# Sliding-window attention and a feed-forward layer on one core: V loads behind the x transposes, q and k transposes before late x, first k loaded by ScalarE

## The chip, the core and the metric

The kernel runs on one core of a Trainium2 chip. Five engines each follow a list of instructions of their own and meet at semaphores: TensorE (PE: matrix products and transposes), ScalarE (ACT: activation functions, copies, casts), VectorE (DVE: element-wise work), GpSimd (POOL) and SyncE (SP). GpSimd, SyncE and ScalarE can also issue DMA transfers. The metric is device time in microseconds for one execution; the time before is 313.18 us, the median of three runs (313.08 to 313.22).

## What is computed

Attention over 8 batches of 8 heads with 576 tokens and 64 values per head, causal with a window of 128 and a bias that falls linearly with distance; its result is rearranged to 4608 tokens of 512 values and goes through two matrix products with g = h cos(h) between them.

```python
scores = scale * q @ k.T                       # per batch and head
bias = slopes * -abs(rel); mask = (rel >= 0) & (rel < 128)
attn = softmax(where(mask, scores + bias, -1e9))
x = (attn @ v).transpose(0, 2, 1, 3).reshape(4608, 512)
h = x @ w_in                                   # 512 -> 2048
out = (h * cos(h)) @ w_out                     # 2048 -> 512
```

## The kernel before

**Tiling and stages.** The 4608 tokens are cut into 9 chunks of 512 for the feed-forward layer. Attention is cut into units: eight for each batch, each a block of queries against itself and the block before it. Seven units of batch 0 run first. Then comes, for each chunk c, the first product (`moe1`, line 748; for chunk 0 `moe1_block`, line 773), 8 or 9 further units of attention (`attention`), and the second product (`moe2`, line 801). In the text, phase c is what is issued between chunk c's first product and its second. The units of phase c are the last one of batch c and the first seven of batch c+1. A unit's scores (line 557) go through an exponential (line 584) and a mask (603) to the product with V (lines 619 to 633), are normalised (656 to 670) into `xnat`, or into `xfirst` for a batch's first block and `xtail` for its last, and must then be transposed into `xT`, the operand of `moe1`.

**The x transposes.** A unit whose tokens are in the first four of a phase (the first two in phase 0) has its x transposed by a DMA on SyncE's queue (`x_dma`, lines 732 and 735); these are collected in the list `begin`. Of the rest, units whose tokens are needed only in the chunk after next ("late x") go through SyncE too; the others are transposed on TensorE (`x_pe`).

**Loads.** Batches 0 and 1 get q and k in pieces (`load_qk`, lines 366 and 377) that TensorE transposes (lines 493 and 498). From batch 2 on, q and k are loaded whole by GpSimd (`load_nat`, line 395, five transfers each for q and k) and transposed by two DMAs each on SyncE's queue (`dma_transposes`, lines 404 and 407; line 404 takes four blocks, line 407 the last half block). In phase c these transposes are for batch c+2, and come after the `begin` transposes; the loads of q and k for batch c+3 wait for them, since they use the same buffer. V of batch c+2 is loaded by GpSimd in five transfers (`load_v`, line 385) into one of two buffers. GpSimd's loads convert float32 to bfloat16 on the way; SyncE's and ScalarE's don't. The first piece of q is loaded as float32 by SyncE and cast by ScalarE or VectorE (line 372).

**What sets the order.** A planner (`Plan.schedule`) simulates the engines with the durations written at each operation (`occ`: the engine is held; `lat`: until the result is there) and at each step starts, for each engine, the ready operation with the smallest priority number, then the earliest in the program. Default priority is 5. The resulting order is fixed at build time for each engine; GpSimd's operations keep the order of the program. At run time each engine follows its list and waits on semaphores for what its next operation reads or overwrites. A planner's duration that is wrong thus changes orders, and not what is waited for. In `op`, a key in `r` makes the operation wait for the writer of that key.

The lines that make the order of V, and of the transposes, in a phase are these:

```python
begin = attention(every[done:done + n], c)
done += n
while next_v < B and done >= 8 * (next_v - 1):
    load_v(next_v)
    next_v += 1
...
    dma_transposes(next_t, begin)
```

Of the kernel before, what the change touches and what calls it, by code (L numbers as in the profile page):

```python
# [8 lines left out]
F32 = mybir.dt.float32  # L9
# [4 lines left out]
NBLK = 5  # L14
# [270 lines left out]
def bass_alibi_sliding__then__act_gcu_kernel(  # L285
# [8 lines left out]
    with ExitStack() as ctx:  # L294
# [4 lines left out]
        op = R.op  # L299
# [2 lines left out]
        w_out = sb("w_outb", [128, NFC, DMODEL])  # L302
        xT = sb("xT", [128, NPAIR, NTOK])
        gT = [sb(f"gT{i}", [128, NFC, CH]) for i in range(2)]
        qF = sb("qfirst", [128, 2, 256], F32)
        qC = sb("qcast", [128, 4, 2, 64])
        qB = {"q": sb("qrows", [128, 2, 1152]), "k": sb("krows", [128, 2, 1152])}
        qE = {"q": sb("qend", [128, 2, 128]), "k": sb("kend", [128, 2, 128])}
        nat = {"q": sb("qnat", [128, NBLK, H, D]), "k": sb("knat", [128, NBLK, H, D])}
# [50 lines left out]
        def load_qk(which, src, b, n=0):  # L360
            t0, rr, _ = PIECES[b][n]
            c0 = 64 * (t0 // 32)
            rows = bass.AP(src.tensor, src[b].offset + 64 * t0,
                           [[64 * rr, 32], [64 * S, H], [1, 64 * rr]])
            if b == 0 and n == 0 and which == "q":
                op("sp", [lambda e: e.dma_start(qF[:, :, :], rows)],
                   w=["qF"], dma="ldqf", occ=400, lat=750)
                i = qF[:, :, :].rearrange("p y (j d) -> p y j d", j=4)
                o = qC[:, :, :, :].rearrange("p j y d -> p y j d")
                op(("act", "dve"),  # L370
                   {"act": lambda e: e.activation(o, i, ACTF.Copy),
                    "dve": lambda e: e.tensor_copy(o, i)},
                   r=["qF"], w=piece_keys(which, b, n), occ={"act": 460, "dve": 330},
                   lat={"act": 560, "dve": 410}, pri=2)
                return
            o = qE[which][:, :, :] if t0 == 512 else qB[which][:, :, c0:c0 + 64 * rr]
            op("pool", [lambda e: e.dma_start(o, rows)],  # L377
               w=piece_keys(which, b, n), dma=f"ld{which}{n}", occ=750,
               lat={2: 600, 4: 1000 if n == 0 else 1050 if which == 'q' else 750,
                    8: 1800 if which == 'q' else 1300, 18: 2850}[rr])  # L380

        def load_v(b, order=range(NBLK)):
            for t in order:
                rows = 128 if t < 4 else 64
                op("pool", [lambda e, t=t, rows=rows: e.dma_start(  # L385
                    vp[b % 2][0:rows, t, :, 0:64],
                    v[b, :, 128 * t:128 * t + rows, :].rearrange("h p d -> p h d"))],
                   r=[("vinit", b % 2)], w=[("v", b % 2, t)], dma=f"ldv{b % 2}{t}",
                   occ=900, lat=7 * rows + (500 if b == 0 and t == 0 else 0))

        def load_nat(which, src, b):
            fns = []
# [7 lines left out]
        def dma_transposes(b, after):  # L400
            for which in ("q", "k"):
                t = tr[which][b % 2][:, :].rearrange("p (c k t) -> p c k t", c=NBLK, k=NPAIR)
                fns = [
                    lambda e, t=t, which=which: e.dma_start_transpose(  # L404
                        t[:, 0:4, :, :].rearrange("p c k t -> p (c k) t"),
                        nat[which][:, 0:4, :, :].rearrange("p c h d -> p (c h d)")),
                    lambda e, t=t, which=which: e.dma_start_transpose(
                        t[:, 4, :, 0:64],
                        nat[which][0:64, 4, :, :].rearrange("p h d -> p (h d)")),
                ]  # L410
                op("sp", fns, r=[("nat", which)] + ([("ktail", b % 2)] if which == "k" else []),
                   w=[("tr", which, b % 2)], dma=f"tr{which}{b % 2}", occ=4500, lat=6500,
                   after=after)

        def load_w_in(f0, f1):
            op("pool", [lambda e: e.dma_start(
# [11 lines left out]
        def constants():  # L428
            op("dve", lambda e: e.memset(zeros[:, :], 0.0), w=["zeros"], occ=60, pri=0)
            op("pool", lambda e: e.iota(dif[:, :, :], pattern=[[128, 2], [-1, 128]], base=-128,  # L430
                                        channel_multiplier=1,
                                        allow_small_or_imprecise_dtypes=True),
               w=["dif"], occ=360)

            op("dve", lambda e: e.tensor_scalar(ident[:, :], dif[:, 1, :], 0.0, None,
                                                ALU.is_equal), r=["dif"], w=["ident"],
               occ=170, lat=250, pri=0)
            for i, (edge, test) in enumerate([(-127.0, ALU.is_lt), (0.0, ALU.is_gt)]):
                op("dve", lambda e, i=i, edge=edge, test=test: e.tensor_scalar(
                    off[:, i, :], dif[:, i, :], edge, -1.0e6, test, ALU.mult),  # L440
                   r=["dif"], w=[("off", i)], occ=170, lat=250, pri=0)
            op("dve", lambda e: e.tensor_tensor(dif[:, :, :], dif[:, :, :], off[:, :, :], ALU.add),
               r=[("off", 0), ("off", 1)], w=["dif"], occ=350, lat=430, pri=0)
            for i in range(2):
                op("dve", lambda e, i=i: e.memset(vp[i][:, :, :, 64:65], 1.0), w=[("vinit", i)],
                   pri=1)
                op("dve", lambda e, i=i: e.memset(vp[i][64:128, 4, :, 0:64], 0.0),
                   w=[("vinit", i)], occ=270, pri=1)
            for i in range(NP):
                op("dve", lambda e, i=i: e.memset(P[i][:, 1024:1088], 0.0), w=[("P", i)], occ=90)  # L450
            op("dve", lambda e: e.memset(halfpi[:, :], math.pi / 2.0), w=["halfpi"], occ=60)
            for i in range(2):
                op("dve", lambda e, i=i: e.memset(
                    tr["k"][i][:, :].rearrange("p (k t) -> p k t", k=NPAIR)[:, :, 576:640], 0.0),
                   w=[("ktail", i)], occ=170)
# [23 lines left out]
        def qk_transposes(b, which, n, part, banks):  # L479
            t0, rr, groups = PIECES[b][n]  # L480
            jj = groups[2 * part:2 * part + 2]
            c0 = 64 * (t0 // 32)
            whole = b == 0 and n == 0 and which == "q"

            def dst(i):
                return ps[:, banks[i], :].bitcast(BF16)[:, 0:128 * (jj[i][1] - jj[i][0])]

            def f(e):
                ins = None
                for i, (j0, j1) in enumerate(jj):  # L490
                    for j in range(j0, j1):
                        if whole:
                            ins = e.transpose(
                                dst(i)[:, 128 * (j - j0):128 * (j - j0) + 128],
                                qC[:, j, :, :].rearrange("p y d -> p (y d)"), ident[:, :])
                            continue
                        for y in range(2):
                            ins = e.transpose(  # L498
                                dst(i)[64 * y:64 * y + 64, 128 * (j - j0):128 * (j - j0) + 128],
                                qE[which][:, y, 64 * j:64 * j + 64] if t0 == 512 else  # L500
                                qB[which][:, y, c0 + 64 * j:c0 + 64 * j + 64], ident[:, :])
                return ins
            num = jj[-1][1] - jj[0][0]
            op("pe", f, r=piece_keys(which, b, n) + ["ident"],
               w=[("B", x) for x in banks[:len(jj)]],
               occ=58 * num, lat=58 * num + 200, mode=0 if whole else 2, pri=3 if b else 2)
            for i, (j0, j1) in enumerate(jj):
                o = tr[which][b % 2][:, :].rearrange("p (k t) -> p k t", k=NPAIR)[
                    :, :, t0:t0 + 32 * rr].rearrange("p k (s j) -> p k s j", j=rr)[:, :, :, j0:j1]
                src_ = dst(i).rearrange("p (j s k) -> p k s j", j=j1 - j0, k=NPAIR)  # L510
                w = 140 * (j1 - j0)
                op(("act", "dve"),
                   {"act": lambda e, o=o, src_=src_: e.activation(o, src_, ACTF.Copy),
                    "dve": lambda e, o=o, src_=src_: e.tensor_copy(o, src_)},
                   w=[("B", banks[i]), ("tr", which, b % 2, t0 + j0)],
                   occ={"act": w + 40, "dve": w + 55}, lat={"act": w + 145, "dve": w + 120},
                   pri=4 if b else 1)
# [371 lines left out]
        for c in range(NCH):  # L889
# [16 lines left out]
            begin = attention(every[done:done + n], c)  # L906
            done += n
            while next_v < B and done >= 8 * (next_v - 1):
                load_v(next_v)
                next_v += 1  # L910
            while next_t < B and done >= 8 * (next_t - 1):
                if next_t < 4:
# [39 lines left out]
```

## Time and profile before

| | us |
|---|---|
| median of three runs | 313.18 |
| the profiled execution | 314.44 |
| its span | 312.5 |
| TensorE busy | 304.3 |
| ScalarE busy | 204.9 |
| VectorE busy | 191.2 |
| GpSimd busy | 97.6 |

The profile is of one execution. The span runs from its first to its last instruction. PE is TensorE's matrix products, PEld its weight loads, which overlap them. "SPq" and "POOLq" are the issuing queues of SyncE and GpSimd, where an issue of a DMA counts with its time on the queue; the transfer itself goes on after that until it lands. In a timeline the columns are start, time, engine, line, operation, out<-in and count, then in brackets the idle time before it and what ended it. In the view of waits they are who waited for whom: total us, times, longest us. The chain of waits is followed back from the last instruction to what released each step. The granted clock of TensorE was 1.0 in the whole span.

### The profile page before, as it was taken

Reading aid. Unit: us, or ns where it says so; the run is one execution under the profiler, and the core shown is the slowest. Engines: PE = TensorE matmul, PEld = TensorE weight load, DVE = VectorE, ACT = ScalarE, POOL = GpSimd, SP = SyncE. Lnnn points to the kernel's source line nnn. Section 1 sums busy time; section 2 is a strip of 40 time slices with the busy share of each in tenths; the row PEclk is TensorE's granted clock in tenths of the full one; section 3 lists DMA queues with packets and bytes.
Section 4 is the critical chain, followed back from the end, with each engine's and each line's share of the span. In section 5 each row is a group of like instructions: output and inputs, shape, how many; then the busy total and the mean of one; then the engine's idle time right before and its main releaser. Section 6 shows DMA issues by size and latency. Waiting matters only on the chain.

```text
span 312.5 us, 6695 instructions
## 1 busy us (share of the span) xinstructions
PE 304.3 (97%) x2722; PEld 160.9 (51%) x2722; DVE 191.2 (61%) x401; ACT 204.9 (66%) x274; POOL 97.6 (31%) x123
## 2 busy tenths in 40 slices
PE   7799999999999999999999999998999999999996
PEld 5589755445544554455444554454445544444444
DVE  5577757585848576858684857576766886353000
ACT  6697866875767677777677667754775878362211
POOL 8998340059122721373054605280000000000000
PEclk9999999999999999999999999999999999999999
DMA  8999999999959996999899999999441320001112
GB/s 104 166 204 206 206 168 188 176 137 169 164 105 162 124 174 106 147 131 138 126 112 181 127 172 82 162 141 178 78 121 44 78 67 2 34 0 69 67 67 101
DMA packets 150333, 38.96 MB, mean 125 GB/s; under 512 B 138912, under 2 KB 145312, under 8 KB 150304
## 3 DMA queue, kind: packets, MB, share of 16 engines
q0 software_dynamic: 100960, 18.23, 76.9%
q1 hardware_dynamic: 49344, 20.33, 32.3%
q8 instruction: 21, 0.34, 0.4%
q14 instruction: 8, 0.07, 0.1%
HBM read 36.70 MB, written 9.44 MB: 148 GB/s over the span
## 4 chain that ended last, share of the span: by engine, by line
PE 83%; DMA 7%; SPq 4%; POOL 3%; ACT 1%; issue 1%; DVE 0%; POOLq 0%; ACTq 0%
PE ps L801 37%; PE ps L748 31%; PE ps L557 5%; PE ps L773 4%; DMA w_inb<-in_moe_w_in_dram 3%; DMA xT<-xfirst 3%; SPq L404 2%; DMA kt<-knat 2%; SPq L735 2%; PE ps L631 1%; PE ps L633 1%; PE ps L619 1%; POOL vp L385 1%; PE ps L498 1%; POOL krows L377 1%
## 5 line engine op out<-in xcount | busy, mean ns | idle before, releaser
L801 PE MATMUL ps<-w_outb,gT 128*128 128x512 bf16 (+2 forms) x592 | 136.5, 374 | 0.0
L748 PE MATMUL ps<-xT,w_inb 128*128 128x512 bf16 x512 | 112.3, 379 | 0.9 <-DMA xT<-xfirst 0.9
L757 DVE TENSOR_TENSOR gT<-ps,cos 128x512 bf16<-128x512 f32 x128 | 86.1, 689 | 41.3 <-ACT cos L753 30.3
L753 ACT ACTIVATE cos<-ps,halfpi 128x512 f32<-128x512 f32 x128 | 85.7, 687 | 23.6 <-PE ps L748 18.8
L584 ACT ACTIVATE p<-ps 128x1024 bf16<-128x1024 f32 x64 | 62.1, 1021 | 29.7 <-PE ps L557 29.5
L801 PEld LDWEIGHTS ps<-w_outb,gT 128*128 128x128 bf16 x592 | 52.9, 98 | 55.4 <-DVE ob L809 0.2
L748 PEld LDWEIGHTS ps<-xT,w_inb 128*128 128x128 bf16 x512 | 49.8, 98 | 61.2 <-issue 1.9
L603 DVE TENSOR_TENSOR p<-p,emask 128x1024 bf16<-128x1024 bf16 x59 | 40.0, 684 | 16.7 <-ACT p L584 16.6
L395 POOL DMA_DIRECT2D qnat<-in_q_dram x30 | 25.3, 877 | 70.0 <-DMA qt<-qnat 70.0
L808 ACT ACTIVATE ob<-ps 128x512 f32<-128x512 f32 (+2 forms) x25 | 14.5, 581 | 41.3 <-PE ps L801 41.2
L385 POOL DMA_DIRECT2D vp<-in_v_dram x40 | 34.0, 895 | 8.4 <-issue 4.3
L395 POOL DMA_DIRECT2D knat<-in_k_dram x30 | 25.4, 881 | 32.6 <-DMA kt<-knat 30.3
L557 PE MATMUL ps<-qt,kt 64*128 64x128 bf16 (+1 forms) x576 | 20.5, 211 | 1.2 <-DMA kt<-knat 0.7
L557 PEld LDWEIGHTS ps<-qt,kt 64*128 64x128 bf16 x576 | 14.6, 94 | 11.7 <-ACT p L584 5.9
L670 DVE TENSOR_TENSOR xnat<-ps,rec 128x256 bf16<-128x256 f32 x48 | 18.3, 419 | 0.4
L773 PE MATMUL ps<-xT,w_inb 128*128 128x128 bf16 x256 | 16.6, 219 | 0.4 <-issue 0.2
L631 PEld LDWEIGHTS ps<-vp,p 128*128 128x128 bf16 x192 | 12.9, 97 | 6.8 <-issue 6.0
L631 PE MATMUL ps<-vp,p 128*128 128x65 bf16 x192 | 15.1, 193 | 0.4 <-DMA vp<-in_v_dram 0.2
L773 PEld LDWEIGHTS ps<-xT,w_inb 128*128 128x128 bf16 x256 | 14.6, 98 | 1.2 <-DMA w_inb<-in_moe_w_in_dram 0.3
L633 PE MATMUL ps<-vp,p 128*128 128x65 bf16 x192 | 15.1, 193 | 0.0
L809 DVE COPY ob<-ps 128x512 f32<-128x512 f32 x12 | 8.2, 680 | 9.8 <-PE ps L801 9.8
L633 PEld LDWEIGHTS ps<-vp,p 128*128 128x128 bf16 x192 | 12.5, 97 | 0.1
(63 smaller groups left out, 158.1 us busy)
## 6 DMA issues: line engine op xcount, KB each, us to landing
out_dram<-ob SPq DMA_DIRECT2D x35, 256.0 KB, 3.7
vp<-in_v_dram POOLq DMA_DIRECT2D x32, 128.0 KB, 7.0
qnat<-in_q_dram POOLq DMA_DIRECT2D x24, 128.0 KB, 6.0
knat<-in_k_dram POOLq DMA_DIRECT2D x24, 128.0 KB, 4.9
w_outb<-in_moe_w_out_dram POOLq DMA_DIRECT2D x4, 512.0 KB, 21.6
w_inb<-in_moe_w_in_dram POOLq DMA_DIRECT2D x3, 512.0 KB, 12.0
qrows<-in_q_dram POOLq DMA_DIRECT2D x1, 576.0 KB, 15.2
krows<-in_k_dram POOLq DMA_DIRECT2D x1, 576.0 KB, 17.3
```

The lines of the kernel that those rows point to most:

```text
L385: op("pool", [lambda e, t=t, rows=rows: e.dma_start(vp[b % 2][0:rows, t, :, 0:64], v[b, :, 128 * t:128 * t + rows, :].rearrange("h p d -> ...
L395: fns.append(lambda e, t=t, rows=rows: e.dma_start(nat[which][0:rows, t, :, :], src[b, :, 128 * t:128 * t + rows, :].rearrange("h p d -> p ...
L557: ins = e.matmul(ps[:, banks[x], c0:c0 + n_], keys_ap(b, x, pr, kc), query_ap(b, x, pr, qb, n_), start=not acc, stop=stop)
L584: op("act", lambda e: e.activation(P[i][:, 0:1024], ps[:, banks[0]:banks[0] + 2, :].rearrange("p a b -> p (a b)"), ACTF.Exp, scale=0.125), ...
L603: op("dve", lambda e: e.tensor_tensor(p, p, m, ALU.mult), r=[("P", i), ("EM", 0), ("EM", 1)], w=[("P", i)], occ=600, lat=690, pri=1)
L631: e.matmul(o, P[i][:, c0:c0 + 128], V[:, qb - 1, h, 0:65], start=True, stop=False)
L633: ins = e.matmul(o, P[i][:, c0 + 128:c0 + 256], V[:, qb, h, 0:65], start=False, stop=True)
L748: op("pe", lambda e, kc=kc: e.matmul(ps[:, bank, :], w_in[:, kc, 128 * fc:128 * fc + 128], xT[:, kc, r0:r0 + CH], start=(kc == 0), stop=(k ...
L753: op("act", lambda e: e.activation(cosb[ci][:, :], ps[:, bank, :], ACTF.Sin, bias=halfpi[:, 0:1]), r=["halfpi"], w=[("B", bank), ("cos", c ...
L757: op("dve", lambda e: e.tensor_tensor(gT[gi][:, fc, :], ps[:, bank, :], cosb[ci][:, :], ALU.mult), r=[("cos", ci)], w=[("B", bank)] + [("g ...
L773: ins = e.matmul(ps[:, bank, 128 * i:128 * i + 128], w_in[:, kc, 128 * fc:128 * fc + 128], xT[:, kc, t0:t0 + 128], start=(kc == 0), stop=( ...
L801: op("pe", lambda e, t=t, fc=fc, bank=bank, j0=j0, j1=j1: e.matmul(ps[:, bank, 0:j1 - j0], gT[gi][:, fc, 128 * t:128 * t + 128], w_out[:, ...
```

## The change

V of a later batch is made to wait for the x transposes in `begin` (the list is handed to `load_v`, and the key of each transpose is added to what the load reads). The DMA transposes of q and k get priority 4. The first piece of k is no longer loaded by GpSimd but, like that of q, as float32 by a hardware queue, k's by ScalarE, then cast and transposed in four wide transposes. The memsets of the second V buffer go behind those of the first, and some planning times are other numbers.

```diff
--- before.py
+++ after.py
@@ -302,8 +302,8 @@
         w_out = sb("w_outb", [128, NFC, DMODEL])
         xT = sb("xT", [128, NPAIR, NTOK])
         gT = [sb(f"gT{i}", [128, NFC, CH]) for i in range(2)]
-        qF = sb("qfirst", [128, 2, 256], F32)
-        qC = sb("qcast", [128, 4, 2, 64])
+        qF = {"q": sb("qfirst", [128, 2, 256], F32), "k": sb("kfirst", [128, 2, 256], F32)}
+        qC = {"q": sb("qcast", [128, 4, 2, 64]), "k": sb("kcast", [128, 4, 2, 64])}
         qB = {"q": sb("qrows", [128, 2, 1152]), "k": sb("krows", [128, 2, 1152])}
         qE = {"q": sb("qend", [128, 2, 128]), "k": sb("kend", [128, 2, 128])}
         nat = {"q": sb("qnat", [128, NBLK, H, D]), "k": sb("knat", [128, NBLK, H, D])}
@@ -362,31 +362,33 @@
             c0 = 64 * (t0 // 32)
             rows = bass.AP(src.tensor, src[b].offset + 64 * t0,
                            [[64 * rr, 32], [64 * S, H], [1, 64 * rr]])
-            if b == 0 and n == 0 and which == "q":
-                op("sp", [lambda e: e.dma_start(qF[:, :, :], rows)],
-                   w=["qF"], dma="ldqf", occ=400, lat=750)
-                i = qF[:, :, :].rearrange("p y (j d) -> p y j d", j=4)
-                o = qC[:, :, :, :].rearrange("p j y d -> p y j d")
+            if b == 0 and n == 0:
+                op("sp" if which == "q" else "act", [lambda e: e.dma_start(qF[which][:, :, :], rows)],
+                   w=[("qF", which)], dma=f"ld{which}f", occ=700,
+                   lat=600 if which == "q" else 400, pri=0)
+                i = qF[which][:, :, :].rearrange("p y (j d) -> p y j d", j=4)
+                o = qC[which][:, :, :, :].rearrange("p j y d -> p y j d")
                 op(("act", "dve"),
                    {"act": lambda e: e.activation(o, i, ACTF.Copy),
                     "dve": lambda e: e.tensor_copy(o, i)},
-                   r=["qF"], w=piece_keys(which, b, n), occ={"act": 460, "dve": 330},
+                   r=[("qF", which)], w=piece_keys(which, b, n), occ={"act": 460, "dve": 330},
                    lat={"act": 560, "dve": 410}, pri=2)
                 return
             o = qE[which][:, :, :] if t0 == 512 else qB[which][:, :, c0:c0 + 64 * rr]
             op("pool", [lambda e: e.dma_start(o, rows)],
                w=piece_keys(which, b, n), dma=f"ld{which}{n}", occ=750,
-               lat={2: 600, 4: 1000 if n == 0 else 1050 if which == 'q' else 750,
-                    8: 1800 if which == 'q' else 1300, 18: 2850}[rr])
-
-        def load_v(b, order=range(NBLK)):
+               lat={2: 600, 4: 800 if which == 'q' else 700,
+                    8: 1700 if which == 'q' else 1300, 18: 2850}[rr])
+
+        def load_v(b, order=range(NBLK), behind=()):
             for t in order:
                 rows = 128 if t < 4 else 64
                 op("pool", [lambda e, t=t, rows=rows: e.dma_start(
                     vp[b % 2][0:rows, t, :, 0:64],
                     v[b, :, 128 * t:128 * t + rows, :].rearrange("h p d -> p h d"))],
-                   r=[("vinit", b % 2)], w=[("v", b % 2, t)], dma=f"ldv{b % 2}{t}",
-                   occ=900, lat=7 * rows + (500 if b == 0 and t == 0 else 0))
+                   r=[("vinit", b % 2)] + [x.w[0] for x in behind], w=[("v", b % 2, t)],
+                   dma=f"ldv{b % 2}{t}",
+                   occ=900, lat=7 * rows + (700 if b == 0 and t == 0 else 0))
 
         def load_nat(which, src, b):
             fns = []
@@ -410,7 +412,7 @@
                 ]
                 op("sp", fns, r=[("nat", which)] + ([("ktail", b % 2)] if which == "k" else []),
                    w=[("tr", which, b % 2)], dma=f"tr{which}{b % 2}", occ=4500, lat=6500,
-                   after=after)
+                   pri=4, after=after)
 
         def load_w_in(f0, f1):
             op("pool", [lambda e: e.dma_start(
@@ -443,9 +445,9 @@
                r=[("off", 0), ("off", 1)], w=["dif"], occ=350, lat=430, pri=0)
             for i in range(2):
                 op("dve", lambda e, i=i: e.memset(vp[i][:, :, :, 64:65], 1.0), w=[("vinit", i)],
-                   pri=1)
+                   pri=i)
                 op("dve", lambda e, i=i: e.memset(vp[i][64:128, 4, :, 0:64], 0.0),
-                   w=[("vinit", i)], occ=270, pri=1)
+                   w=[("vinit", i)], occ=270, pri=i)
             for i in range(NP):
                 op("dve", lambda e, i=i: e.memset(P[i][:, 1024:1088], 0.0), w=[("P", i)], occ=90)
             op("dve", lambda e: e.memset(halfpi[:, :], math.pi / 2.0), w=["halfpi"], occ=60)
@@ -480,7 +482,7 @@
             t0, rr, groups = PIECES[b][n]
             jj = groups[2 * part:2 * part + 2]
             c0 = 64 * (t0 // 32)
-            whole = b == 0 and n == 0 and which == "q"
+            whole = b == 0 and n == 0
 
             def dst(i):
                 return ps[:, banks[i], :].bitcast(BF16)[:, 0:128 * (jj[i][1] - jj[i][0])]
@@ -492,7 +494,7 @@
                         if whole:
                             ins = e.transpose(
                                 dst(i)[:, 128 * (j - j0):128 * (j - j0) + 128],
-                                qC[:, j, :, :].rearrange("p y d -> p (y d)"), ident[:, :])
+                                qC[which][:, j, :, :].rearrange("p y d -> p (y d)"), ident[:, :])
                             continue
                         for y in range(2):
                             ins = e.transpose(
@@ -906,7 +908,7 @@
             begin = attention(every[done:done + n], c)
             done += n
             while next_v < B and done >= 8 * (next_v - 1):
-                load_v(next_v)
+                load_v(next_v, behind=begin)
                 next_v += 1
             while next_t < B and done >= 8 * (next_t - 1):
                 if next_t < 4:
```

## The prediction

> **What bounds the kernel now.** I read the page first, then who TensorE waits for, then the busy time of each engine by stretch.
>
> ```profile
> span 312.5 us, 6695 instructions
> PE 304.3 (97%) x2722; PEld 160.9 (51%) x2722; DVE 191.2 (61%) x401; ACT 204.9 (66%) x274; POOL 97.6 (31%) x123
> ```
>
> ```profile
> PE ps L748 <- DMA xT<-xfirst: 0.9, 1, 0.9
> PE ps L557 <- DMA kt<-knat: 0.7, 1, 0.7
> PE ps L619 <- DMA vp<-in_v_dram: 0.5, 1, 0.5
> PE ps L773 <- DMA w_inb<-in_moe_w_in_dram: 0.2, 1, 0.2
> ```
>
> ```profile
> 8.00:13.00 5.00, 3.56 (x68) 2.07 (x64) 2.89 (x7) 3.64 (x5) 5.00 (x7) 1.00 1.44 166
> 13.00:18.00 5.00, 4.62 (x100) 3.35 (x96) 3.24 (x12) 3.83 (x5) 5.00 (x8) 1.00 1.67 186
> 22.00:310.00 288.00, 286.25 (x2444) 147.77 (x2441) 177.24 (x350) 188.09 (x252) 76.77 (x92) 1.00 1.09 123
> ```
>
> In the last view the columns are the stretch, its length, then the busy time of PE, PEld, DVE, ACT and POOL, the granted clock, the DMA share and GB/s. The reader is to see that TensorE is the bound: from 22 to 310 us it works 286.25 of 288.00 us at full clock, so all idle time there is 1.75 us, and two waits, one for the k transposes (0.7) and one for the x transpose of a batch's first block (0.9), are nearly all of it. Before 22 us TensorE waits for arriving data (3.56 of 5 us busy from 8 to 13). Since it never catches up later, whatever is cut from those two waits, or from the time at which the first weights arrive, comes off the end one for one; whatever adds a wait costs the same. Nothing else in the change can move the time.
>
> The two waits sit in one stretch of the chain of waits (columns: start, us, what), and the SyncE queue shows how they come about.
>
> ```profile
> 104.56 0.58 PE ps L557 x24
> ...
> 136.00 0.58 PE ps L557 x24
> ...
> 195.33 5.61 DMA kt<-knat
> ...
> 200.98 0.63 PE ps L557 x24
> ...
> 209.51 8.37 DMA xT<-xfirst
> ...
> 217.97 13.97 PE ps L748 x64
> ```
>
> ```profile
> 89.74 2.53 SPq L735 DMA_TRANSPOSE xT<-xnat  x2
> 92.31 3.57 SPq L404 DMA_TRANSPOSE kt<-knat  x1
> ...
> 121.84 3.01 SPq L735 DMA_TRANSPOSE xT<-xnat  x2
> 124.90 3.99 SPq L404 DMA_TRANSPOSE kt<-knat  x1
> ...
> 185.82 5.13 SPq L735 DMA_TRANSPOSE xT<-xnat  x4
> 191.00 4.28 SPq L404 DMA_TRANSPOSE kt<-knat  x1
> 195.33 1.24 SPq L407 DMA_TRANSPOSE kt<-knat  x1
> ...
> 224.47 1.84 SPq L404 DMA_TRANSPOSE kt<-knat  x1
> 226.36 1.82 SPq L407 DMA_TRANSPOSE kt<-knat  x1
> ```
>
> I call a phase c what comes after chunk c's first matmul. In phase 4 four late x transposes occupy SyncE's queue from 185.82, so the k transposes start at 191.00 and land at 200.94 (195.33 + 5.61). TensorE was ready 0.7 us before that.
>
> **Part 1, q and k transposes ahead of late x (pri 4).** SyncE picks by priority among what is ready. The late x were ready when the k transposes began to be eligible (they were issued), so with pri 4 the order turns round. The k transposes move up by 92.31 - 89.74 = 2.57 us in phase 1, 124.90 - 121.84 = 3.06 in phase 2 and 191.00 - 185.82 = 5.18 in phase 4. The late x move down by the two issues of k, 4.28 + 1.24 = 5.5 us in phase 4; their issues end near 196.5. Their blocks are needed only at L748 of the chunk after next, in phase 4 the one at 217.97: that 20 us is what hides them. Were that cover gone, each would cost what it is late. Gain: 0.7, as 5.18 is far more than 0.7.
>
> **Part 2, V behind the first x.** GpSimd's queue shows what surrounds the wait for xfirst.
>
> ```profile
> 103.17 4.20 POOL L395 DMA_DIRECT2D knat<-in_k_dram  x5 [7.45 <-DMA kt<-knat]
> ...
> 134.66 4.20 POOL L395 DMA_DIRECT2D knat<-in_k_dram  x5 [6.95 <-DMA kt<-knat]
> ...
> 201.47 4.20 POOL L395 DMA_DIRECT2D knat<-in_k_dram  x5 [8.24 <-DMA kt<-knat]
> 205.60 4.24 POOL L385 DMA_DIRECT2D vp<-in_v_dram  x5
> ```
>
> The transpose of xfirst issued at 209.51 took 8.37 us, with five loads of V issued up to 209.84 and five of k ahead of them. One phase later, where nothing is loaded, the same transpose is seen alone:
>
> ```profile
> L732 SPq DMA_TRANSPOSE xT<-xfirst x1: 1190/1190/1190, 243.0 to 243.0; - x1
> ...
> DMA to landing us min/median/max: 2.5/2.5/2.5
> ```
>
> With V held back the transpose takes between 2.5 and 8.37 us. It needs to be only 0.9 shorter, and by part 1 the knat loads move up too, as they wait for the k transposes (201.47 is 0.53 after 200.94). So I take the wait as gone: 0.9. If V were not held, 0.9 stays.
>
> What is queued behind the waiting GpSimd instruction: the five V loads themselves, then the qnat and knat loads. These wait for the q and k transposes in any case, which stand behind the first x in SyncE's queue, so they lose at most the 4.24 us of V's issues. For phase 4 V is used only after the scores at 200.98 (L557), more than 10 us past the point where V's loads would be issued. The wait itself costs nothing while that cover holds.
>
> The risk is where V now goes: beside the q and k transposes. The price of sharing comes from two phases. In phase 4, with qnat loads beside it, the k pair takes 200.94 - 191.00 = 9.9 us. In phase 5, with none, it is 226.36 + 2.9 - 224.47 = 4.8, by this landing row of its two transposes (the lower is the second's):
>
> ```profile
> DMA to landing us min/median/max: 2.9/3.7/4.4
> ```
>
> So one set of five loads costs the pair 5.1 us. Call the added delay by V D: it lies between 0 (the pair was already sharing with qnat, and V only takes qnat's place) and 5.1 (V comes on top). I take D between 0 and 2, since in the phases that matter qnat's share is already in the landing times. What can be borne: the landing in phase 1 is 103.17 - 0.53 = 102.64 with use at 104.56, so 1.92, and with the 2.57 gained, 4.49; in phase 2, 136.00 - 134.13 + 3.06 = 4.93; in phase 4, 5.18 - 0.63 = 4.55. All exceed 2, so no new wait.
>
> [...]
>
> **Part 3, first k by ScalarE's queue, and the start.** The start's chain runs along GpSimd's issues to the first weights.
>
> ```profile
> 1.26 0.85 POOL L377 DMA_DIRECT2D krows<-in_k_dram  x1 [0.82 <-POOLq L937]
> ...
> 2.50 0.71 POOL L377 DMA_DIRECT2D qrows<-in_q_dram  x1
> ...
> 9.66 2.27 POOL L416 DMA_DIRECT2D w_inb<-in_moe_w_in_dram  x3
> ```
>
> ```profile
> krows<-in_k_dram POOLq DMA_DIRECT2D x1, 128.0 KB, 3.3
> ```
>
> ```profile
> 9.66 8.44 DMA w_inb<-in_moe_w_in_dram
> ```
>
> ```profile
> 4.00:4.50 0.50, 0.22 (x1) 0.10 (x1) 0.50 (x4) 0.50 (x3) 0.50 (x1) 1.00 0.58 61
> ```
>
> Removed: one GpSimd load (0.85 us). All later GpSimd issues move up by 0.85 to, at most, 2.50 - 1.26 = 1.24 us (if the iota fits into the setup ahead of them). Added: one issue on ScalarE, one cast and a larger write (256 KB in place of 128).
>
> ```profile
> 0.74 0.74 SPq L366 DMA_DIRECT2D qfirst<-in_q_dram  x1
> ```
>
> ```profile
> 5.04 0.38 DVE L372 CAST qcast<-qfirst 128x512 bf16<-128x512 f32 x1
> ```
>
> ```profile
> 3.73 1.33 ACT L469 ACTIVATE bias<-dif 128x256 bf16<-128x256 f32 x4 [1.70 <-DVE dif L442]
> ```
>
> The issue on ScalarE is priced by q's on SyncE, 0.74; it stands ahead of the table load and is hidden by the 1.70 us that ScalarE then waits for dif, which itself comes earlier. The cast (0.38) and four wide transposes for eight narrow ones lie ahead of the first scores; after them TensorE waits for V anyway (0.5 at L619), and that covers the 0.38. If the cover went, 0.38 is lost. The order of the memsets and the changed planning times alter only orders in this stretch; I price them with it.
>
> What the earlier issues bring is bounded from both sides. Best: all arrivals follow, 1.24 us off. Worst: the transfers and not the issues set the arrivals, and the additional 128 KB at 166 to 186 GB/s costs 0.7 us. The delay from issue to landing grows from 3.3 (first load) to 8.44 us, which speaks for transfers; the share of 0.58 at 4.0 to 4.5 us shows a hole into which loads could move. I take 0.3 gained, the middle.
>
> **The sum.** 0.7 + 0.9 + 0.3 = 1.9 us. The profiled execution has a span of 312.5 inside 314.44 us, 1.94 around it; it would become 310.6 and 312.5. The runs' median, 313.18, is 1.26 below that profiled time; the same 1.9 makes it **311.3 us**.
>
> **Rivals.**
> 1. V takes the place of the wait: D = 5.1. Then phases 1, 2 and 4 wait 5.1 - 4.49 = 0.6, 0.2 and 0.55, 1.3 in all, and 313.18 - 1.6 + 1.3 - 0.3 = 312.6. For: the factor of two between phases 4 and 5. Against: qnat is already in phase 4.
> 2. The start loses: 313.18 - 1.6 + 0.7 = 312.3. For: transfers bound arrivals there. Against: the hole at 4 us.
> 3. Slower: V in the k transposes' way with more than its own price, because it slows the q transposes ahead of them too, and k then starts late. Place: the scores (L557) that use the k of phases 1, 2 and 4. The three can bear 4.49 + 4.93 + 4.55 = 13.97 together, so the waits are 3D - 13.97, and from D = 5.3 on these exceed the 1.9 gained. At D = 6.2 it gives 3 x 6.2 - 13.97 = 4.6 us of waits against 1.9 gained: 315.9. For: V now starts exactly when the q transposes do. Against: D would have to exceed the whole measured price.
> 4. The start neither gains nor loses: transfers alone set the arrivals, k's transfer is only moved from one queue to another, and the additional bytes fit into the hole. 313.18 - 1.6 = 311.6. For: the growth to 8.44. Against: the hole itself, which shows that the transfers were not yet the limit at 4 us.
> 5. It doesn't do what it says: the planner puts late x ahead as before, or V's wait ends before it matters. Then 313.2. Against: late x and k were both ready, so pri decides.
>
> [...]
>
> **How the numbers follow.** Chances: forecast 0.45, rival 4 0.17, rival 1 0.12, rival 2 0.10, rival 3 0.09, rival 5 0.07. The range takes the best start, 313.18 - 1.6 - 1.24 = 310.4, and at the upper end rival 5 and the worst start together with little of the middle, 313.3; beyond it lies rival 3. A measurement of this kernel tells 0.2% (0.63 us) from no change, so faster means below 312.55: nearly all of the forecast and of rival 4, about half of rival 1 and most of rival 2, 0.73; slower is rival 3, 0.09; the same, 0.18.
>
> **What would show it.** Right: no wait of TensorE at L748 for xT or at L557 for kt; in SyncE's queue L404 and L407 of k directly behind those of q, then L735; GpSimd's V loads after the landing of the first x; the first rows of GpSimd's loads about 1 us earlier and the wait for w_inb ending before 18.10. Wrong: a new wait at L557 in any phase (rivals 1 and 3), waits at L619 or L631 for vp past 50 us (V too late), a later first w_inb (rival 2).

## The result and the profile after

The changed kernel took 311.13 us (median of six runs, 310.58 to 311.58) against 313.2 us for the kernel before (six runs, 312.86 to 313.48); the ratio is 0.9944, with a 95% interval of 0.9921 to 0.9968. The profiled execution took 311.13 us. These are the head of its page and who TensorE waited for (total us, times, longest):

```profile
span 309.3 us, 6639 instructions
...
PE 301.1 (97%) x2675; PEld 161.4 (52%) x2717; DVE 189.9 (61%) x400; ACT 205.6 (66%) x276; POOL 97.2 (31%) x122
```

```profile
PE ps L573 <- DVE bias L472: 1.1, 1, 1.1
...
PE ps L803 <- issue: 1.0, 6, 0.2
PE ps L621 <- ACT p L586: 0.4, 1, 0.4
```

(The lines of the code have moved by two: 748 is now 750, 557 is 559, 404 is 406, 735 is 737, 801 is 803.) Neither xT nor kt appears any more; both waits are gone. I read the six waits "issue" of 0.2 us as products missing from the trace (2675 products against 2717 weight loads), and not as time lost.

SyncE's queue in phases 4 and 5, with the two issues of k, then the late x, then the x of the next batch's first block:

```profile
179.86 6.32 SPq L406 DMA_TRANSPOSE kt<-knat  x1
186.22 1.25 SPq L409 DMA_TRANSPOSE kt<-knat  x1
188.00 5.07 SPq L737 DMA_TRANSPOSE xT<-xnat  x4
...
203.67 1.21 SPq L734 DMA_TRANSPOSE xT<-xfirst  x1
```

GpSimd's queue at the start and in phase 4:

```profile
1.35 0.84 POOL L378 DMA_DIRECT2D qrows<-in_q_dram  x1 [0.17 <-issue]
...
8.80 2.27 POOL L418 DMA_DIRECT2D w_inb<-in_moe_w_in_dram  x3
...
177.77 4.19 POOL L386 DMA_DIRECT2D vp<-in_v_dram  x5 [12.45 <-DMA xT<-xnat]
186.87 4.19 POOL L397 DMA_DIRECT2D qnat<-in_q_dram  x5 [4.91 <-DMA qt<-qnat]
192.53 4.20 POOL L397 DMA_DIRECT2D knat<-in_k_dram  x5 [1.47 <-DMA kt<-knat]
```

The order of k and late x has turned round, V waits 12.45 us for the last of the first x, and the load of knat, which stood at 201.47, goes out at 192.53. The time from issue to landing of the x transpose at 203.67, and of k's second one at 186.22:

```profile
L734 SPq DMA_TRANSPOSE xT<-xfirst x1: 1214/1214/1214, 203.7 to 203.7; - x1
...
DMA to landing us min/median/max: 2.5/2.5/2.5
```

```profile
L409 SPq DMA_TRANSPOSE kt<-knat x1: 1252/1252/1252, 186.2 to 186.2; - x1
...
DMA to landing us min/median/max: 5.8/5.8/5.8
```

The x transpose took 8.37 us before and takes 2.5 now. k lands at 192.0, 12.1 us after its issue, where the pair took 9.9 before: V is in its way, but TensorE uses k only at 193.95. TensorE's order is a new one, too. These are its first products with that k, and the first of chunk 6, where it waited for that x before:

```profile
193.95 0.63 PE L559 MATMUL ps<-qt,kt 64*128 64x64 bf16 x24
...
207.33 1.24 PE L750 MATMUL ps<-xT,w_inb 128*128 128x512 bf16 x5
```

Chunk 6 begins 3.66 us after the issue of that transpose. Before, TensorE was there 7.56 us after it (217.97 - 0.90 - 209.51). So the new order needs the short landing: at 8.37 us TensorE would wait 4.7 us here.

At the start the first large part of w_in, issued at 8.80 and not at 9.66, lands 7.9 us later, at 16.7 instead of 18.1:

```profile
w_inb<-in_moe_w_in_dram POOLq DMA_DIRECT2D x1, 256.0 KB, 7.9
```

**A measure for the parts.** TensorE's orders differ from kernel to kernel, but the first product of chunk 1 (the first row of L748 or L750 with 128x512) ends the start in all of them. Before and after it stands here:

```profile
55.93 2.32 PE L748 MATMUL ps<-xT,w_inb 128*128 128x512 bf16 x10
```

```profile
54.64 3.62 PE L750 MATMUL ps<-xT,w_inb 128*128 128x512 bf16 x16
```

The two profiled executions differ by 1.29 us up to there, and by (312.5 - 55.93) - (309.3 - 54.64) = 256.57 - 254.66 = 1.91 us in the rest. The same split for every kernel of the experiments:

| kernel | first product of chunk 1 | rest of the span | ratio to before, 95% interval |
|---|---|---|---|
| before | 55.93 | 256.57 | |
| before, again | 56.46 | 255.34 | 1.0033 [1.0001, 1.0064] |
| priority 4 alone | 55.50 | 255.10 | 0.9975 [0.9956, 0.9994] |
| V wait alone | 55.25 | 254.65 | 0.9953 [0.9926, 0.9980] |
| priority 4 and V wait | 56.48 | 254.72 | 0.9961 [0.9942, 0.9980] |
| start alone | 54.65 | 256.85 | 0.9975 [0.9951, 0.9998] |
| start and priority 4 | 54.26 | 255.44 | 0.9942 [0.9924, 0.9960] |
| start and V wait | 56.08 | 254.62 | 0.9932 [0.9909, 0.9956] |
| the change | 54.64 | 254.66 | 0.9944 [0.9921, 0.9968] |
| the change, again | 54.65 | 254.75 | 0.9926 [0.9908, 0.9944] |
| planned for the V wait, without it | 55.24 | 254.96 | 0.9977 [0.9958, 0.9995] |
| first k by SyncE | 57.55 | 254.45 | 1.0012 [0.9992, 1.0033] |
| two first pieces | 56.47 | 254.53 | 1.0006 [0.9984, 1.0028] |
| more filler | 54.95 | 254.75 | 0.9954 [0.9939, 0.9970] |

The columns 2 and 3 are of one profiled execution each. The kernel before against itself came out at 1.0033, so differences of 0.3% between two ratios tell nothing here.

### The profile page after: what moved, and what is told of

Read it like the earlier page. It is cut to its first block, busy times and chain, and to the rows that moved or that the text cites. A ratio compares the mean times of both kernels' runs of the same rounds, so it can differ in the third digit from the quotient of the medians.

```text
span 309.3 us, 6639 instructions
## 1 busy us (share of the span) xinstructions
PE 301.1 (97%) x2675; PEld 161.4 (52%) x2717; DVE 189.9 (61%) x400; ACT 205.6 (66%) x276; POOL 97.2 (31%) x122
## 4 chain that ended last, share of the span: by engine, by line
PE 96%; issue 1%; DVE 1%; ACT 1%; POOL 0%; ACTq 0%; POOLq 0%
PE ps L803 40%; PE ps L750 35%; PE ps L559 6%; PE ps L775 5%; PE ps L633 2%; PE ps L635 2%; PE ps L500 2%; PE ps L621 2%; PE ps L573 1%; PE ps L712 1%; PE ps L625 1%; DVE gT L759 0%; ACT cos L755 0%; ACT p L586 0%; PE ps L495 0%
## 5 line engine op out<-in xcount | busy, mean ns | idle before, releaser
L803 PE MATMUL ps<-w_outb,gT 128*128 128x512 bf16 (+2 forms) x563 | 130.7, 373 | 2.1 <-issue 1.0
L750 PE MATMUL ps<-xT,w_inb 128*128 128x512 bf16 x501 | 112.4, 379 | 0.6
L755 ACT ACTIVATE cos<-ps,halfpi 128x512 f32<-128x512 f32 x128 | 85.7, 687 | 25.9 <-PE ps L750 17.9
L750 PEld LDWEIGHTS ps<-xT,w_inb 128*128 128x128 bf16 x512 | 49.5, 98 | 59.2 <-issue 1.1
L811 DVE COPY ob<-ps 128x512 f32<-128x512 f32 x11 | 7.5, 682 | 8.1 <-PE ps L803 8.1
```

The source lines that it names most:

```text
L750: op("pe", lambda e, kc=kc: e.matmul(ps[:, bank, :], w_in[:, kc, 128 * fc:128 * fc + 128], xT[:, kc, r0:r0 + CH], start=(kc == 0), stop=(k ...
L755: op("act", lambda e: e.activation(cosb[ci][:, :], ps[:, bank, :], ACTF.Sin, bias=halfpi[:, 0:1]), r=["halfpi"], w=[("B", bank), ("cos", c ...
L803: op("pe", lambda e, t=t, fc=fc, bank=bank, j0=j0, j1=j1: e.matmul(ps[:, bank, 0:j1 - j0], gT[gi][:, fc, 128 * t:128 * t + 128], w_out[:, ...
```

## The experiments

**Parts alone.** The first four ran on one chip.

The start alone (the change without these two):

```diff
-                   pri=4, after=after)
+                   after=after)
...
-                load_v(next_v, behind=begin)
+                load_v(next_v)
```

> The change's start (first k by ScalarE, memset order, planning times) without the V wait and without priority 4. Theory A, the start is worth what the profile after shows: at the row L775 x88 that stands at 25.00 before and 23.90 after, TensorE is 1.1 us ahead and nothing gives it back, so 1.1 us faster, ratio 0.9965, with the waits for kt and xfirst still there. Theory B, the prediction's terms: 0.3 us faster, ratio 0.999; what the trace shows as 1.1 is given back at the first waits for data. Theory C: the start alone makes the late waits longer, since x and k transposes meet V and knat as before while TensorE arrives earlier: no change, ratio 1.000.

Measured: 0.9975, 313.14 us. TensorE's waits for data in its profile:

```profile
PE ps L559 <- DMA kt<-knat: 1.0, 2, 0.7
...
PE ps L750 <- DMA xT<-xfirst: 0.5, 1, 0.5
...
PE ps L750 <- DMA xT<-xnat: 0.3, 1, 0.3
```

TensorE is as early at chunk 1 as in the change (54.65), and then waits 1.8 us for x and k, which left the rest at 256.85. This is theory A for the start and C for the rest: what the start brings is partly given back while the late waits are there. The wait for xfirst follows its landing: 8.4 us from issue to landing in the first profile and a wait of 0.9, 7.9 here and 0.5, and 6.8 with no wait when the kernel before is run again (below).

Priority 4 alone, and the V wait alone, each on the kernel before:

```diff
                    w=[("tr", which, b % 2)], dma=f"tr{which}{b % 2}", occ=4500, lat=6500,
-                   after=after)
+                   pri=4, after=after)
```

> Before with priority 4 on the q and k transposes alone. Theory A: the wait of 0.7 us at L557 for kt is gone, the wait for xfirst stays or shrinks as the knat loads move up by 2.5 to 5 us, 0.7 to 1.6 us faster in a run that had both waits. Theory B: the median runs of before have smaller waits than its profiled run (314.44 against 313.18), so 0.3 us or less.

```diff
-                load_v(next_v)
+                load_v(next_v, behind=begin)
```

> Before with V's loads behind the first x transposes alone. Theory A: the wait for xfirst (0.9) goes and the one for kt (0.7) stays or grows, since V now lands beside the k transposes that still stand behind late x: 0 to 0.9 us faster. Theory B (the prediction's slower rival): V's price of up to 5.1 us comes on top of landings that have 0.4 to 1.9 us to spare, so new waits at L557 in several phases, 1 to 4 us slower.

Measured: 0.9975 and 0.9953, and neither profile has a wait for kt or xT. In each, theory A is nearest, but both waits are gone where it left one. Priority 4 thus also removed the wait for xfirst, though V doesn't wait in this kernel. Its x transpose at 205.40 landed in 2.5 us, because GpSimd's loads that had lain beside it went out earlier, as knat waits for the k transposes:

```profile
L732 SPq DMA_TRANSPOSE xT<-xfirst x1: 1189/1189/1189, 205.4 to 205.4; - x1
...
DMA to landing us min/median/max: 2.5/2.5/2.5
```

```profile
191.04 4.20 POOL L395 DMA_DIRECT2D knat<-in_k_dram  x5 [1.05 <-DMA kt<-knat]
195.17 2.69 POOL L385 DMA_DIRECT2D vp<-in_v_dram  x3
201.43 1.57 POOL L385 DMA_DIRECT2D vp<-in_v_dram  x2 [3.57 <-PE ps L623]
```

With the V wait alone, k lands late: issued at 196.08, 6.6 us to landing, 202.7 where the kernel before had 200.94. TensorE still doesn't wait, since its order is another:

```profile
198.14 4.91 PE L801 MATMUL ps<-w_outb,gT 128*128 128x512 bf16 x22
202.99 0.63 PE L557 MATMUL ps<-qt,kt 64*128 64x64 bf16 x24
```

Before the change the same place has nine such products and then the wait:

```profile
198.21 2.10 PE L801 MATMUL ps<-w_outb,gT 128*128 128x512 bf16 x9
200.98 0.63 PE L557 MATMUL ps<-qt,kt 64*128 64x64 bf16 x24 [0.67 <-DMA kt<-knat]
```

In the planner's model a transpose on SyncE is delayed by the loads issued ahead of it (the `wire` term in `schedule`). With V there it should expect k later, and it puts 22 instead of nine products ahead of the scores; that the one causes the other is read from its code and not tested.

The kernel before, unchanged:

> The kernel before, once more. It tells whether the two waits of the first profile (0.7 for kt, 0.9 for xfirst) belong to every run or to that one, which was 1.26 us above the median. Theory A: both come again within 0.5 us of their size. Theory B: one or both are absent, and the middle of the kernel was worth less than 1.6 us in the runs. The time is that of before, ratio 1.000.

Measured: a wait of 0.4 us for kt and none for a transfer into xT; span 311.8. So the wait for kt came back smaller and the one for xfirst not at all (theory B): their size depends on the run. The rest is 255.34 here and 256.57 in the first profile, whose execution was 1.26 us above the median.

**Pairs.** The next four ran together on one chip (before: 313.55 us, 17 runs).

The change without the V wait:

```diff
-                load_v(next_v, behind=begin)
+                load_v(next_v)
```

> The change without the V wait. Theory A (what priority 4 alone showed): the k transposes land early, so GpSimd's knat and V loads are issued some 10 us earlier and are off the wire before the first x; both waits of the middle stay away, and the time is that of the whole change within 0.3 us, ratio near 0.994. Theory B (the prediction's): the wait for xfirst is V's doing and comes back, 0.5 to 0.9 us slower than the change.

The change without priority 4:

```diff
-                   pri=4, after=after)
+                   after=after)
```

> The change without priority 4. Theory A: the V wait alone also takes both waits away, because x lands in 2.5 us; the time is that of the whole change within 0.3 us. Theory B: with the start moved up by 1.1 us TensorE reaches the scores before k is there, as in the start alone (1.0 us at L557's place for kt); 0.5 to 1 us slower than the change.

Priority 4 and the V wait on the kernel before, that is both of the single edits above:

> The change without the start. Theory A: priority 4 and the V wait remove the same waits, so together they bring what either brings alone, 0.8 to 1.5 us against before, and the whole change owes its remaining 1 us to the start: about 1 us slower than the change. Theory B: they add up, 2 us or more against before, and the start brings under 0.3.

The change once more:

> The whole change beside the three pairs on one chip. Theory A: ratio 0.994 as first measured, with no wait of TensorE for kt or xT in its profile and a narrower spread of runs than before (1.0 us against 0.6 to 5). Theory B: the first ratio was luck of one chip; waits as in the start alone.

Measured: 311.84, 311.37, 312.63 and 311.18 us. In the rest of the span every kernel with the V wait has 254.45 to 254.75, with priority 4 or without; with priority 4 and without the V wait it is 255.1 and 255.4; with neither 255.3 to 256.9. So in these profiles the V wait does all that is to be had in the middle, priority 4 does a part of it and adds nothing beside the V wait. Without the V wait (the first), theory A is right that both waits stay away, but its median is 0.66 us above the change's, in the band of theory B and outside the 0.3 of A. The two intervals overlap, so the time doesn't settle it; the profiles have 0.69 us more in the rest of the span (255.44 against 254.75), and not as a wait for kt or xT. Without priority 4 (the second), it is 0.19 us, as theory A says. The third agrees with theory A: 313.55 - 312.63 = 0.92 us for the two edits together. The change itself has no wait for kt or xT again. What the start adds to the pair is 312.63 - 311.18 = 1.45 us by the medians; the twelve runs of the whole change in both its sets lie between 310.58 and 311.64. That this is narrower than before isn't shown: the kernel before spread over 0.6 us in its first set and over more in the others.

**The wait or the plan?** The change with each engine's order as planned for it, where the V loads don't wait for x at run time:

```diff
+        for o, xs in freed:
+            for x in xs:
+                o.preds.pop(x)
         R.emit(final=[f"st{i}" for i in range(NOB)])
```

(`freed` holds each V load with its list of x transposes.)

> The whole change with every engine's order exactly as planned for it, but GpSimd does not wait for the first x before V's loads; only the plan knows of it. Theory A: the waits of TensorE went because its order was planned anew around earlier x and k; without the run-time wait V's loads go out right behind knat, xfirst lands in 4 us and not 2.5, k's pair in 8 and not 12, and the time is that of the change within 0.3 us. Theory B: the run-time wait itself keeps the x transposes quick; TensorE, whose order now expects x early, waits 0.5 to 2 us for xT in one or more phases.

Measured: 312.15 us, 0.9977. No wait for kt or xT in the profile; k's pair of phase 4 goes from 180.71 to a landing at 187.6 (183.91 and the 3.7 below), 6.9 us, where the change had 12.1 with V beside it:

```profile
L412 SPq DMA_TRANSPOSE kt<-knat x1: 1252/1252/1252, 183.9 to 183.9; - x1
...
DMA to landing us min/median/max: 3.7/3.7/3.7
```

The rest of the span is 254.96, 0.3 above the change and below all kernels that were planned without the V wait, though only by 0.14 us. So in this execution the new plan, with priority 4, carried nearly all of the middle's gain, and the run-time wait 0.3 us. Priority 4 alone already gets V out of the way early, and it does here: V's loads go out from 192.41, and the x transpose of 204.50 lands in 2.4 us. What the plan is worth without priority 4 wasn't tried. By the medians the kernel is 0.8 us behind the one with more filler (311.36, below, on the same chip), so theory A's 0.3 us isn't met, while theory B's waits are absent. Of the profile's difference from the change 0.6 us lies before chunk 1, where both kernels have the same orders, so that part is the start's spread and not the wait. How much of the median belongs to the wait stays open.

**The start.** The first k by SyncE's queue, behind q:

```diff
-                op("sp" if which == "q" else "act", [lambda e: e.dma_start(qF[which][:, :, :], rows)],
+                op("sp", [lambda e: e.dma_start(qF[which][:, :, :], rows)],
```

> The change with the first k issued by SyncE's queue behind q instead of by ScalarE's. Theory A: what the start gains is GpSimd's 0.9 us, as w_in's arrival moved with GpSimd's issues (18.1 before, 16.7 after); k lands some 0.5 us later, which the cast's slack takes; the time is that of the change within 0.3 us. Theory B: ScalarE's queue of its own matters; k lands 0.7 us later, the first scores move with it, 0.3 to 0.7 us slower than the change.

Measured: 313.31 us, 1.0012: against 311.36 for the kernel with more filler on the same chip, about 2 us more. Both theories fell short. The first loads' times from issue to landing, here and in the change:

```profile
qfirst<-in_q_dram SPq DMA_DIRECT2D x1, 256.0 KB, 3.2
kfirst<-in_k_dram SPq DMA_DIRECT2D x1, 256.0 KB, 4.8
```

```profile
qfirst<-in_q_dram SPq DMA_DIRECT2D x1, 256.0 KB, 4.0
kfirst<-in_k_dram ACTq DMA_DIRECT2D x1, 256.0 KB, 3.3
```

k is issued at 1.53 instead of 0.75 and lands at 6.3 instead of 4.05, 2.3 us later for 0.8 us of issue; TensorE waits for its cast:

```profile
PE ps L495 <- DVE kcast L373: 0.8, 1, 0.8
```

and the start ends at 57.55, 2.9 us after the change's. The w_in load lands at 16.0, earlier than in the change. So an earlier w_in alone brought nothing here: the first k itself came late, which the queue of its own avoids. Of the 2.9 us the profile shows 0.8 as this wait. The rest isn't taken apart: TensorE came late to full rate in this execution (at about 14 us, told below), and its order from about 11 us on is another than the change's, since this kernel is planned anew. How much of the 2 us between the medians is the queue's, and how much the order's, stays open; the next kernel has that same order from there on.

The second pieces of q and k by the two hardware queues, too:

```diff
-            if b == 0 and n == 0:
+            if b == 0 and n < 2:
...
-            whole = b == 0 and n == 0
+            whole = b == 0 and n < 2
```

(with a buffer for each piece)

> The change with the second pieces of q and k, too, as float32 by SyncE and ScalarE, so that GpSimd issues two loads fewer (1.5 us). Theory A, issues set the arrivals: w_in's first large load is issued at 7.2 and lands at 15.2 instead of 16.7, up to 1.4 us faster than the change. Theory B, transfers set them: w_in lands at 16.3 or later, and TensorE, at half rate until about 9 us or later, cannot use it; within 0.3 us of the change, or slower by the two additional casts (0.4 to 0.7 us each on VectorE or ScalarE ahead of the first scores).

Measured: 312.71 us, 1.0006. w_in is issued at 8.83 (8.80 in the change), as V's first load, now the first of GpSimd's, waits 1.7 us for its memset; it lands at 15.5, 1.2 us earlier than in the change; the start still ends 1.8 us later, at 56.47. TensorE stands still for 1.28 us near 20 us:

```profile
20.09 0.20 PE L633 MATMUL ps<-vp,p 128*128 128x65 bf16 x1 [1.28 <-issue]
```

Earlier arrivals were not worth anything to this order of TensorE, which is also the order of the kernel with k by SyncE. Neither theory was tried as meant, as w_in's issue did not move to 7.2; neither names the stall, and its cause wasn't followed further.

More filler at the start (24 and 8 products in place of 17 and 6):

```diff
-    FILL = 107
+    FILL = 75
```

> The change with 24 and 8 filler matrix products at the start instead of 17 and 6, which close the gap of 1.07 us ahead of the first bias product. In the profiles TensorE goes to full rate (128-column products at 219 and not 314 ns) at about 7, 9 or 14 us for the same program. Theory A: the gap is why it sometimes happens late; with it closed the early switch comes each time, the profile's row L775 x88 stands at 23.5 to 23.9, runs spread less, median 0 to 0.5 us below the change. [...]

Measured: 311.36 us (310.59 to 311.96), 0.9954: no difference from the change that these intervals could show. TensorE was at full rate from 7.23 us in its profile, and then waited 0.6 us for w_in, which landed at 17.6 there: with TensorE early, the data seem to set the end of the start (54.95). Theory A is right about the early switch in this one execution, and its gain isn't there. No kernel of these is clearly faster than the change.

## Why the prediction was right, and where its terms were off

The time was forecast as 311.3 us and came out at 311.13, in the way that was forecast: both waits are gone and the first loads are earlier. The terms fared differently.

1. **TensorE is the bound: right. Gains come off the end one for one: right only for the edits together.** With the waits gone, the 1.29 us of the start are still there at the end: the spans differ by 3.2, 1.91 of it in the rest. But in the start alone TensorE was as early at chunk 1 and then lost 1.8 us to waits for x and k, so most of the start's gain did not reach the end. And the two waits are not two separate prices, as the next point shows.
2. **Part 1, 0.7 us for the wait for kt, and part 2, 0.9 for the one for xfirst: the sum right in kind, the assignment wrong.** The step that failed is "If V were not held, 0.9 stays": priority 4 alone took both waits away: knat, and behind it the first three of V's five loads, go out 10 us earlier (V at 195.17 against 205.60), and the x transpose lands in 2.5 us. And the V wait alone took both away as well. Beside it priority 4 has no effect on the rest of the span (254.7 with it, 254.6 without). The sizes were read from one execution that stood 1.26 us above the median; in the second profile of the same kernel the rest was 1.2 us shorter. The terms were thus upper values for a usual run.
3. **D, V's delay of the k transposes, taken between 0 and 2: short.** The pair took 12.1 us in phase 4 against 9.9 before, so D is 2.2, and by the same reading 1.5 in phase 1 and 2.8 in phase 2. All are below the 4.5 that could be borne, and no wait arose; rivals 1 and 3 needed 5.1 and more. This D is a net figure, as priority 4 also shortens the pair: it took 7.9 us in phase 4 with priority 4 alone and 12.7 with priority 4 and the V wait, so V itself costs 4.8 there. That V only takes qnat's place (D of 0) thus did not hold: in the change V's loads go out from 177.77, qnat's from 186.87, and the pair, from 179.86 to 192.0, meets both. The working also left out that the place where TensorE uses k isn't fixed: the planner moved it, from 200.98 to 193.95 in the change and to 202.99 with the V wait alone. So the 4.5 was no measure of the room; in the change 1.9 us are left in phase 4 (193.95 - 192.0).
4. **Part 3, 0.3 us, "the middle" of -1.24 and +0.7: too small.** w_in's arrival moved by 1.4 us (18.1 to 16.7) for 0.86 of issue in the first pair of profiles; in the other profiles it lies at 17.7 to 17.9 without the new start and at 16.7 to 17.6 with it (k by SyncE and two first pieces left aside). So neither the loss by the larger write nor the 0 of rival 4 came about. Between the profiles the start brought 1.29; over the executions in which TensorE came to full rate early the start ends at 55.25, 55.50 and 55.93 without the new start, and at 54.26 to 55.24 in five with it (start alone, start and priority 4, the change twice, planned for the V wait): 55.56 and 54.69 on average, 0.9 us. The cast of k is covered: the change's profile has no wait for it, and behind the first scores TensorE stands 0.4 us for ScalarE's p (L621), where the prediction expected it to wait for V. With k 2.3 us later the cover was gone, and TensorE waited 0.8 us.
5. **The total:** a middle read too large and a start read too small made up for each other. By the medians of one chip, priority 4 and the V wait bring 0.92 us where the sum had 1.6, and the start adds 1.45 where it had 0.3 (with whatever the executions differ by in TensorE's rate at the start, told below). That the time was met within 0.2 us is luck; the sign and the mechanism rest on the experiments.

Rival 5 (the order stays) is excluded by SyncE's rows. Nothing was tried in which D passes the room, so the point from which rival 3 decides was not measured.

## What to carry to other kernels

Where transfers wait for one another or share the wire in a ring (k transposes, then knat, then V, then x, then k), cutting any one link may free all of them. Here priority 4 alone and the V wait alone each left neither the wait of 0.7 us nor that of 0.9, and with priority 4 alone the x transpose landed in 2.5 us and not in the 8.37 that it took beside the loads. So price edits together and not one by one, and test each alone. Where a planner lays out the order, an edit moves the places where data are needed as well as the times at which they land: compare the two in the new order, and not the new landing with the old place. And read the size of a small wait from more than one execution.

## What the hardware showed that was not expected

**TensorE's rate at the start differs from run to run.** The same group of sixteen narrow transposes in the change, and in the change without priority 4, whose start has the same orders:

```profile
10.92 0.64 PE L500 MATMUL ps<-ident,qrows 128*64 128x128 bf16 x16
```

```profile
11.54 1.06 PE L500 MATMUL ps<-ident,qrows 128*64 128x128 bf16 x16
```

A product takes 219 ns in the one and 314 ns in the other, while the granted clock reads 1.00 in both. The full rate begins between about 7 us (the first profile, more filler) and about 14 us (before again, priority 4 and V wait, start and V wait, k by SyncE), and it shows in the table: with the late switch the start ends at 56.08 to 57.55, otherwise at 54.26 to 55.93 (two first pieces, at 56.47, switched early and lost its time in a stall). In that state the new start brings only 56.47 - 56.08 = 0.4 us (the mean of before again and priority 4 and V wait, against the one execution of start and V wait). This fits TensorE's own rate being the limit there, and not the data, but one execution doesn't show it. What sets the time of the switch is not shown: in the change and in the change without priority 4 the same orders switch at about 9.5 us and at about 14 us.

**A second hardware queue brought k earlier by more than its issue.** With k behind q on SyncE's queue, q took 0.8 us less to land than with k beside it on ScalarE's (3.2 against 4.0). But k landed 2.3 us later (6.3 against 4.05) for an issue 0.8 us later (1.53 against 0.75), so the queue of its own brought k 1.5 us earlier beyond the issue (one execution with k on SyncE's queue; with k on ScalarE's it took 3.2 to 3.5 us in every profile of the same loads). Here the measured landing decides.
